# Placeholder products pinned behind the causal-mask products, and the first unit's maximum queued ahead of the second's

## Chip, cores and metric

The kernel runs on one core of a Trainium2 chip. The metric is device microseconds of one execution, from launch to end; three executions of the kernel before took 603.52, 604.0 and 604.48 us (median 604.0). Everything else comes from one profiled execution, in which the hardware recorded each instruction of each engine.

## What is computed

Causal attention, then two feed-forward stages, all in float32 precision:

```python
scores = scale * q @ k.T                       # 2 batches, 12 heads, 448 rows, head size 64
scores = where(upper triangle, -1e9, scores)   # causal mask
attn = exp(scores - rowmax) / (rowsum + 1e-9)
x = (attn @ v), heads side by side             # 896 x 768
h = x @ w_in; g = piecewise-quadratic(h); y = g @ w_out        # inner width 2048
out = (silu(y @ w_gate) * (y @ w_val)) @ w_out2                # inner width 1536
```

## The kernel before

The program is written in the order of a software pipeline, and a planner (the framework's scheduler) turns it into one instruction queue for each engine. An engine takes its queue strictly in order. The planner moves an instruction ahead of earlier written ones when, by its own estimate of time, the engine would stand idle otherwise. Two things limit it: an instruction that reads or overwrites data of an earlier one stays behind that one, and `tc.keep_in_program_order(op)` keeps `op` behind whatever was written last for the same engine. The helper `follow` (line 78) issues a product that way, at raised priority, unless its second argument (`first`) is true.

Attention is cut into units of two heads. For the first 12 steps (`j == 0`) a step is one unit's first 224 query rows; later steps (`j == 2`, `3`) take the rest, two steps a unit. The loop at line 505 runs over `k`, and each pass issues pieces of four neighbouring steps in the order of the table `ORDER` (line 54). In the first 12 passes the list is: `scores(k+1)`, `greatest(k+1)` (the word `max`), the filler, `values(k-2)`, `normalize(k)`, `turn(k-1)`, `exps(k+1)`; the copy `turned(k-2)` stands at the head.

- `scores` (line 338), on TensorE: four float32 products of queries and keys (each is two records of the profile), then four bf16 products of the mask with an identity (lines 353 to 359), which add the mask to the diagonal blocks. They read `mask_b`, made by GpSimd at line 481, and `ident_b`, made by VectorE at line 485. The result lies in one of two PSUM tiles `s`, so that `scores(k+2)` has to wait until `exps(k)` has read `scores(k)`.
- `greatest` (line 362), on VectorE: two row maxima and one multiplication by -1/8.
- `exps` (line 374), on ScalarE: four exponentials, each followed by a read of its row sums.
- `normalize` (line 388), on VectorE; `turn` (line 410), six transposes on TensorE; `turned` (line 420), a copy on ScalarE; `values` (line 429), the products with v on TensorE; `x_hi` and `x_lo`, the split of their result.

TensorE has nothing useful as filler in the first passes. `zeros(n)` (line 471) then issues `n` products of a zero tile into a PSUM bank that nobody reads (line 473): `zeros(WARM)` gives eight ahead of everything else, and passes k = 0 to 13 give 12, 6, 4 and then 2 each (`HOLD`, line 31), 44 in all. They are written without a pin. From pass 14 on the filler is a quarter of a real product of the first feed-forward stage. Weights arrive as two int32 halves of a float64 and are narrowed by three VectorE instructions (lines 99 to 105) before they are split in two (lines 195 and 196); the first two tiles' first instruction is pinned.

A step's scores products are called S0, S1, ... in this text, its mask products M0, M1, ..., its transposes T0, ..., its products with v V0, ...

Of the kernel before, what the change touches and what calls it, by code (L numbers as in the profile page):

```python
# [13 lines left out]
ALU = mybir.AluOpType  # L14
AX = mybir.AxisListType
# [6 lines left out]
C = 112  # L22
# [5 lines left out]
HALF = DM // 2  # L28
WB = 768
WARM = 8  # L30
HOLD = (12, 6, 4, 2)
AHEAD = 3
LASTB = 2
WBUFS = 4
# [29 lines left out]
def fused_kernel(ctx: ExitStack, tc: tile.TileContext, qk, v, w_in, w_out, w_gv, w_o2, out):  # L64
    nc = tc.nc
# [12 lines left out]
    def follow(product, first, *args, **kw):  # L78

        if first:  # L80
            return product(*args, **kw)  # L81
        with tc.high_priority():
            return tc.keep_in_program_order(product(*args, **kw))  # L83
# [178 lines left out]
    def bank():  # L262
        pool = banks.pop(0)
        banks.append(pool)
        return pool.tile([128, 512], F32, tag="mm", name="mm")
# [46 lines left out]
    with ExitStack() as ph:  # L312
# [25 lines left out]
        def scores(k):  # L338

            u, j = steps[k]  # L340
            qk_t, _ = ld[u]
            s = ps_s.tile([128, 2, 512], F32, tag="s", name="s")
            k0 = GT if j == 0 else 0

            for i, (off, w, q0) in enumerate(reversed(SEGS[j])):
                for h in range(2):
                    hd = slice(h * D, (h + 1) * D)
                    follow(
                        nc.tensor.matmul, i == h == 0,
                        out=s[:C, h, off:off + w], lhsT=qk_t[hd, q0:q0 + C], rhs=qk_t[hd, k0:k0 + w],  # L350
                        start=(i == 0), stop=False, skip_group_check=True,
                    )
            for off, w, _ in SEGS[j]:
                for h in range(2):
                    follow(
                        nc.tensor.matmul, False,
                        out=s[:C, h, off + w - C:off + w], lhsT=ident_b[:C, :], rhs=mask_b[:C, :],
                        start=False, stop=True, skip_group_check=True,
                    )
            st[k] = {"s": s}  # L360

        def greatest(k):

            _, j = steps[k]
            s, segs = st[k]["s"], SEGS[j]
            mx = s[:C, 0, 504:508].rearrange("p (i h) -> p i h", h=2)
            for i, (off, w, _) in enumerate(segs):
                nc.vector.tensor_reduce(out=mx[:, i], in_=s[:C, :, off:off + w], axis=AX.X, op=ALU.max)  # L368
            m = pp.tile([C, 2, 2], F32, tag="mx", name="mx")
            nc.vector.tensor_scalar(  # L370
                out=m[:, :len(segs)], in0=mx[:, :len(segs)], scalar1=-0.125, scalar2=None, op0=ALU.mult)
            st[k]["mx"] = m

        def exps(k):

            _, j = steps[k]
            s, mx = st[k]["s"], st[k]["mx"]
            sm = pp.tile([C, 2, 2], F32, tag="sm", name="sm")
            p = pp.tile([C, 2, S], F32, tag="p", name="p")
            for i, (off, w, _) in enumerate(SEGS[j]):  # L380
                for h in range(2):
                    nc.scalar.activation(  # L382
                        out=p[:, h, off:off + w], in_=s[:C, h, off:off + w], func=AF.Exp,
                        bias=mx[:, i, h:h + 1], scale=0.125, accum_out=sm[:, i, h:h + 1],
                    )
            st[k].update(p=p, sm=sm)

        def normalize(k):
            _, j = steps[k]
            p, segs = st[k]["p"], SEGS[j]  # L390
            sm = st[k].pop("sm")
            m = sm[:, :len(segs)]
            nc.vector.tensor_scalar(out=m, in0=m, scalar1=1e-9, scalar2=None, op0=ALU.add)
            nc.vector.reciprocal(out=m, in_=m)
            for i, (off, w, _) in enumerate(segs):
                if j == 0 and NORM_P:
                    nc.gpsimd.tensor_tensor(
                        out=p[:, :, off:off + w], in0=p[:, :, off:off + w],
                        in1=sm[:, i].unsqueeze(2).to_broadcast([C, 2, w]), op=ALU.mult,
                    )  # L400
                else:
                    norms = NORM0 if j == 0 else NORM1
                    for h in range(2):
                        ph, r = p[:, h, off:off + w], sm[:, i, h:h + 1]
                        if norms[(2 * k + h) % len(norms)] == "V":
                            nc.vector.tensor_scalar(out=ph, in0=ph, scalar1=r, scalar2=None, op0=ALU.mult)  # L406
                        else:
                            nc.scalar.mul(out=ph, in_=ph, mul=r)

        def turn(k):  # L410
            u, j = steps[k]
            p = st[k]["p"]
            t = ps_t.tile([128, 2, 512], F32, tag="t", name="t")
            for h in range(2):
                for i in range(NK[j]):
                    sl = slice(i * C, (i + 1) * C)
                    follow(nc.tensor.transpose, i == 0, t[:C, h, sl], p[:, h, sl], ident[:C, :C])
            st[k]["t"] = t

        def turned(k):  # L420
            u, j = steps[k]
            if j != 3:
                pts[u] = pp.tile([C, 2, 784], F32, tag="pt", name="pt", bufs=2)
            off, w = (336 if j == 3 else 0), NK[j] * C
            turns = TURN0 if j == 0 else TURN1
            (nc.vector.tensor_copy if turns[k % len(turns)] == "V" else nc.scalar.copy)(
                out=pts[u][:, :, off:off + w], in_=st[k].pop("t")[:C, :, :w])
# [30 lines left out]
        def x_hi(o, xh, xl):  # L458
            nc.scalar.copy(out=xh, in_=o)
            return o, xh, xl  # L460
# [6 lines left out]
        idle = lp.tile([128, 512], BF16, name="idle", bufs=1)  # L467
        nc.vector.memset(idle, 0.0)
        warm = bank()

        def zeros(n):
            for _ in range(n):
                nc.tensor.matmul(out=warm, lhsT=idle[:, :128], rhs=idle, start=True, stop=True)  # L473

        zeros(WARM)
        make_identity(nc, ident)
        nc.vector.memset(mask_b, 0.0)
# [4 lines left out]
            out=mask_b[:C, :], in_=mask_b[:C, :], compare_op=ALU.is_ge, fill=MASK,  # L482
# [22 lines left out]
        for k in range(-1, last + 2):  # L505
            lead, lag = k + 1 < last, k - 2 >= 0
            pv = lag and steps[k - 2][1] != 2
            kind = 0 if k < first1 else 2 + (k - first1) % 2
            for op in ORDER[kind]:
                if op == "copy" and lag:  # L510
                    turned(k - 2)
                elif op == "scores" and lead:
                    scores(k + 1)
                elif op == "max" and lead:
                    greatest(k + 1)
                elif op == "exp" and lead:
                    exps(k + 1)
                elif op == "norm" and 0 <= k < last:
                    normalize(k)
                elif op == "turn" and 0 <= k - 1 < last:  # L520
                    assert "t" not in st.get(k - 2, ())
                    turn(k - 1)
                elif op == "values" and pv:
                    assert not fresh_o and not half_o and "t" not in st[k - 2]
                    fresh_o.append(values(k - 2))
                elif op == "x_hi" and fresh_o:
                    half_o.append(x_hi(*fresh_o.pop()))
                elif op == "x_lo" and half_o:
                    x_lo(*half_o.pop())
                elif op == "fill" and k >= 0:  # L530
                    if k >= first1 + 2:
                        filler()
                    else:
                        zeros(HOLD[min(k, len(HOLD) - 1)])
                elif op == "relu" and fresh:
                    half.append(h_relu(*fresh.pop()))
                elif op == "square" and half:
                    whole.append(h_max(*half.pop()))
                elif op == "g_hi" and whole:
                    split_h.append(g_hi(*whole.pop()))  # L540
                elif op == "g_lo" and split_h:
                    g_lo(*split_h.pop())
                elif op == "weights" and k >= 2:
                    W.tick((TICKS if k < first1 else LATER)[k % 3])
            if lead and steps[k + 1][1] != 3:
                load(steps[k + 1][0] + AHEAD)
            if k == 0:
                W.load(2)
# [191 lines left out]
    for hf in range(2):  # L740
# [14 lines left out]
        for i in range(last):  # L755
            w = W.get(I_O2 + hf * NB + i)
# [58 lines left out]
```

## Time and profile before

| | |
|---|---|
| median of three executions | 604.0 us (603.52 to 604.48) |
| profiled execution, its own time | 603.42 us |
| its span, first to last instruction | 601.6 us |
| TensorE (PE) busy | 593.4 us, 99% |
| TensorE weight load (PEld) busy | 521.3 us, 87% |
| VectorE (DVE) busy | 441.5 us, 73% |
| ScalarE (ACT) busy | 232.4 us, 39% |
| attention passes | about 4.7 to 140 us of the span |

Times in the rows below are in us from the start of the span, durations in us unless ns is written. A timeline row gives the start, the duration, the engine, the line, the operation, output and inputs by name, shapes, and how many instructions were merged into it. Matmuls overlap in the pipeline, so a record's duration is longer than the distance to the next one's start; the pace is read from the starts. Products issued through `follow` carry line 81 or 83 (the helper), the zero products line 473.

### The profile page before, as it was taken

Reading aid. Unit: us, or ns where it says so; the run is one execution under the profiler, and the core shown is the slowest. Engines: PE = TensorE matmul, PEld = TensorE weight load, DVE = VectorE, ACT = ScalarE, POOL = GpSimd, SP = SyncE. Lnnn points to the kernel's source line nnn. Section 1 sums busy time; section 2 is a strip of 40 time slices with the busy share of each in tenths; the row PEclk is TensorE's granted clock in tenths of the full one; section 3 lists DMA queues with packets and bytes.
Section 4 is the critical chain, followed back from the end, with each engine's and each line's share of the span. In section 5 each row is a group of like instructions: output and inputs, shape, how many; then the busy total and the mean of one; then the engine's idle time right before and its main releaser. Section 6 shows DMA issues by size and latency. Waiting matters only on the chain.

```text
span 601.6 us, 8762 instructions
## 1 busy us (share of the span) xinstructions
PE 593.4 (99%) x3334; PEld 521.3 (87%) x3334; DVE 441.5 (73%) x811; ACT 232.4 (39%) x499; POOL 117.1 (19%) x68
## 2 busy tenths in 40 slices
PE   9999999999999999999999999999999999999997
PEld 5766667668999999999999999999999999999997
DVE  3999999872886777666874699489787899863401
ACT  3987777653344433111121454224224342512100
POOL 0000000000311221323133212124122233632300
PEclk9999999999999999999999999999999999999999
DMA  8575554300151234567644303133333333544002
GB/s 260 175 212 171 172 176 151 106 1 1 53 158 33 84 93 150 182 210 245 194 133 146 106 1 105 53 105 106 103 111 103 105 106 115 200 157 145 1 1 92
DMA packets 23417, 72.52 MB, mean 121 GB/s; under 512 B 2640, under 2 KB 9616, under 8 KB 23376
## 3 DMA queue, kind: packets, MB, share of 16 engines
q1 hardware_dynamic: 20784, 69.61, 36.7%
q10 hardware_dynamic: 2592, 2.36, 1.1%
q8 instruction: 26, 0.43, 0.3%
q14 instruction: 15, 0.12, 0.1%
HBM read 66.85 MB, written 5.11 MB: 120 GB/s over the span
## 4 chain that ended last, share of the span: by engine, by line
PE 84%; DVE 13%; ACT 1%; DMA 1%; issue 0%; ACTq 0%
PE mm L81 34%; PE mm L660 27%; PE mm L749 5%; PE mm L751 5%; PE mm L750 5%; DVE s L368 3%; DVE p L406 2%; PE mm L83 2%; PE s L81 1%; DVE wt L105 1%; DVE wt L102 1%; PE mm L473 1%; ACT p L382 1%; DVE wl L196 1%; DMA wraw<-w_in 1%; PE t L83 1%
## 5 line engine op out<-in xcount | busy, mean ns | idle before, releaser
L196 POOL TENSOR_TENSOR wl<-wt,wh 128x768 fp32r<-128x768 f32 (+1 forms) x52 | 102.5, 1976 | 428.3 <-ACT wh L195 428.3
L195 ACT CAST wh<-wt 128x768 fp32r<-128x768 f32 (+1 forms) x61 | 49.7, 816 | 152.0 <-DVE wt L105 40.7
L99 DVE TENSOR_SCALAR wt<-wraw 128x768 int32<-128x768 int32 (+1 forms) x64 | 44.9, 701 | 41.8 <-POOL wl L196 36.7
L102 DVE SCALAR_TENSOR_TENSOR wt<-wraw,wt 128x768 int32<-128x768 int32 (+1 forms) x64 | 72.5, 1132 | 0.8
L81 PE MATMUL mm<-gh,wh 128*128 128x448 f32 x192 | 70.1, 365 | 0.0
L81 PE MATMUL mm<-gh,wl 128*128 128x448 f32 x192 | 70.1, 365 | 0.0
L81 PE MATMUL mm<-gl,wh 128*128 128x448 f32 x192 | 70.1, 365 | 0.0
L660 PE MATMUL mm<-yl,wh 128*128 128x448 f32 x180 | 65.7, 365 | 0.0
L660 PE MATMUL mm<-yh,wl 128*128 128x448 f32 x180 | 65.7, 365 | 0.0
L660 PE MATMUL mm<-yh,wh 128*128 128x448 f32 x180 | 65.7, 365 | 0.0
L105 DVE SCALAR_TENSOR_TENSOR wt<-wraw,wt 128x768 int32<-128x768 int32 (+1 forms) x64 | 64.4, 1007 | 0.7
L81 PE MATMUL mm<-xh,wh 128*128 128x448 f32 x165 | 62.6, 379 | 2.4 <-DVE q L288 2.4
L749 PE MATMUL mm<-wh,uh 128*128 128x384 f32 x168 | 56.1, 334 | 0.0
L750 PE MATMUL mm<-wl,uh 128*128 128x384 f32 x168 | 56.1, 334 | 0.0
L751 PE MATMUL mm<-wh,ul 128*128 128x384 f32 x168 | 56.1, 334 | 0.0
L382 ACT ACTIVATE p<-s,mx 112x112 f32<-112x112 f32 (+3 forms) x96 | 46.4, 497 | 20.0 <-DVE mx L370 14.4
L81 PE MATMUL mm<-xl,wh 128*128 128x448 f32 x138 | 50.4, 365 | 0.0
L81 PE MATMUL mm<-xh,wl 128*128 128x448 f32 x138 | 50.2, 365 | 0.0
L368 DVE TENSOR_REDUCE s<-s 112x2 f32<-112x224 f32 (+3 forms) x48 | 35.4, 743 | 6.9 <-PE s L83 6.7
L81 PEld LDWEIGHTS mm<-gl,wh 128*128 128x128 f32 x192 | 36.1, 188 | 2.9
L81 PEld LDWEIGHTS mm<-gh,wl 128*128 128x128 f32 x192 | 36.1, 188 | 2.9
L81 PEld LDWEIGHTS mm<-gh,wh 128*128 128x128 f32 x192 | 36.1, 188 | 2.8
(132 smaller groups left out, 1216.8 us busy)
## 6 DMA issues: line engine op xcount, KB each, us to landing
wraw<-w_gv SPq DMA_DIRECT2D x18, 768.0 KB, 4.3
wraw<-w_in SPq DMA_DIRECT2D x16, 768.0 KB, 4.7
wraw<-w_out SPq DMA_DIRECT2D x12, 768.0 KB, 4.6
wraw<-w_o SPq DMA_DIRECT2D x12, 768.0 KB, 4.2
araw<-w_gv SPq DMA_DIRECT2D x18, 256.0 KB, 4.8
qk_t<-qk SPq DMA_DIRECT2D x12, 336.0 KB, 3.2
wraw<-w_out SPq DMA_DIRECT2D x6, 512.0 KB, 3.8
qk_t<-qk SPq DMA_DIRECT2D x12, 224.0 KB, 3.9
```

The costliest lines, as they stand in the source:

```text
L81: return product(*args, **kw)
L99: yield nc.vector.tensor_scalar(out=t, in0=w[:, :, 1], scalar1=3, scalar2=0x3FFFFFF8, op0=ALU.logical_shift_left, op1=ALU.bitwise_and,)
L102: yield nc.vector.scalar_tensor_tensor(out=t, in0=w[:, :, 1], scalar=-0x40000000, in1=t, op0=ALU.bitwise_and, op1=ALU.bitwise_or,)
L105: yield nc.vector.scalar_tensor_tensor(out=t, in0=w[:, :, 0], scalar=29, in1=t, op0=ALU.logical_shift_right, op1=ALU.bitwise_or,)
L195: nc.scalar.copy(out=wh[:, :n], in_=t)
L196: (nc.vector if i < LOW_V else nc.gpsimd).tensor_tensor(out=wl[:, :n], in0=t, in1=wh[:, :n].bitcast(F32), op=ALU.subtract,)
L368: nc.vector.tensor_reduce(out=mx[:, i], in_=s[:C, :, off:off + w], axis=AX.X, op=ALU.max)
L382: nc.scalar.activation(out=p[:, h, off:off + w], in_=s[:C, h, off:off + w], func=AF.Exp, bias=mx[:, i, h:h + 1], scale=0.125, accum_out=sm ...
L660: nc.tensor.matmul(out=ps[:, :N], lhsT=w[a][:, sl], rhs=rows[c][b], start=(first and c == i == 0), stop=(last and c == i == 2), skip_group ...
L749: nc.tensor.matmul(out=ps, lhsT=c, rhs=a, start=(f == 0), stop=False)
L750: nc.tensor.matmul(out=ps, lhsT=c, rhs=b, start=False, stop=False)
L751: nc.tensor.matmul(out=ps, lhsT=d, rhs=a, start=False, stop=(f == FC2 - 1))
```

## The change

`HOLD` gives 9 instead of 12 zero products in pass 0. The zero products of passes 0, 1 and 2 are pinned in program order: nine behind M1, six behind M2, four behind M3. The first product of S1 is pinned too, so that all of S1 lies behind M0. The maxima and the negation of steps 0 and 1 are pinned on VectorE, in the order written.

```diff
-HOLD = (12, 6, 4, 2)
+HOLD = (9, 6, 4, 2)
...
                     follow(
-                        nc.tensor.matmul, i == h == 0,
+                        nc.tensor.matmul, i == h == 0 and k != 1,
                         out=s[:C, h, off:off + w], lhsT=qk_t[hd, q0:q0 + C], rhs=qk_t[hd, k0:k0 + w],
...
             for i, (off, w, _) in enumerate(segs):
-                nc.vector.tensor_reduce(out=mx[:, i], in_=s[:C, :, off:off + w], axis=AX.X, op=ALU.max)
+                largest = nc.vector.tensor_reduce(out=mx[:, i], in_=s[:C, :, off:off + w], axis=AX.X, op=ALU.max)
+                if k < 2:
+                    tc.keep_in_program_order(largest)
             m = pp.tile([C, 2, 2], F32, tag="mx", name="mx")
-            nc.vector.tensor_scalar(
+            negate = nc.vector.tensor_scalar(
                 out=m[:, :len(segs)], in0=mx[:, :len(segs)], scalar1=-0.125, scalar2=None, op0=ALU.mult)
+            if k < 2:
+                tc.keep_in_program_order(negate)
...
-        def zeros(n):
+        def zeros(n, pin=False):
             for _ in range(n):
-                nc.tensor.matmul(out=warm, lhsT=idle[:, :128], rhs=idle, start=True, stop=True)
+                op = nc.tensor.matmul(out=warm, lhsT=idle[:, :128], rhs=idle, start=True, stop=True)
+                if pin:
+                    tc.keep_in_program_order(op)
...
-                        zeros(HOLD[min(k, len(HOLD) - 1)])
+                        zeros(HOLD[min(k, len(HOLD) - 1)], k < len(HOLD) - 1)
```

## Rows read from the trace of the kernel before

**Rows 1.** View by windows: stretch, length, PE, PEld, DVE, ACT, POOL busy, clock, DMA, GB/s.

```profile
5.00:16.00 11.00, 11.00 (x90) 7.00 (x89) 5.74 (x23) 4.99 (x24) 0.00 (x0) 1.00 0.92 300
16.00:63.00 47.00, 46.72 (x394) 31.46 (x392) 46.67 (x151) 39.94 (x134) 0.00 (x0) 1.00 0.63 195
63.00:112.00 49.00, 47.60 (x328) 32.71 (x327) 48.57 (x120) 34.44 (x81) 0.00 (x0) 1.00 0.50 151
112.00:145.00 33.00, 31.16 (x212) 22.98 (x212) 19.88 (x51) 17.87 (x43) 0.00 (x0) 1.00 0.08 25
145.00:597.00 452.00, 452.00 (x2304) 424.96 (x2303) 319.43 (x464) 133.65 (x220) 116.14 (x61) 1.00 0.35 112
```

**Rows 2.** The same view for the zero products alone: PE, PEld, clock, DMA, GB/s.

```profile
0.00:5.00 5.00, 3.60 (x8) 1.04 (x8) 1.00 0.53 143
5.00:12.00 7.00, 5.47 (x24) 2.22 (x24) 1.00 1.01 337
12.00:20.00 8.00, 0.04 (x1) 0.00 (x0) 1.00 0.63 193
```

**Rows 3.** Timeline of TensorE, 4.7 to 12 us.

```profile
4.71 0.50 PE L81 MATMUL s<-qk_t 64*112 64x224 f32 x1
...
5.51 0.44 PE L81 MATMUL s<-qk_t 64*112 64x224 f32 x1
...
6.28 1.68 PE L473 MATMUL mm<-idle 128*128 128x512 bf16 x7
7.80 0.58 PE L83 MATMUL s<-mask_b,ident_b 112*112 112x112 bf16 x8
...
8.21 3.83 PE L473 MATMUL mm<-idle 128*128 128x512 bf16 x17
```

**Rows 4.** Timeline of VectorE and ScalarE in the same stretch; in brackets, what ended idle time.

```profile
8.36 1.76 DVE L368 TENSOR_REDUCE s<-s 112x2 f32<-112x224 f32 x4 [6.75 <-PE s L83]
10.03 0.29 DVE L370 TENSOR_SCALAR mx<-s 112x4 f32<-112x4 f32 x2
10.28 0.35 ACT L382 ACTIVATE p<-s,mx 112x112 f32<-112x112 f32 x1 [8.05 <-DVE mx L370]
...
11.95 0.17 DVE L393 TENSOR_SCALAR sm<-sm 112x4 f32<-112x4 f32 x1 [1.64 <-ACT p L382]
```

**Rows 5.** Timeline of GpSimd and VectorE: the last writers of the mask products' operands.

```profile
1.26 0.28 POOL L481 TENSOR_SCALAR_AFFINE_SELECT mask_b<-mask_b 112x112 bf16<-112x112 bf16 x1
1.34 0.28 DVE L485 CAST ident_b<-ident 128x112 bf16<-128x112 f32 x1
```

**Rows 6.** Timeline of TensorE, 11.9 to 20 us: first rows of S2, M2, T0, S3, S4, S5.

```profile
11.97 0.44 PE L81 MATMUL s<-qk_t 64*112 64x224 f32 x1
...
12.73 0.41 PE L83 MATMUL s<-mask_b,ident_b 112*112 112x112 bf16 x4
12.98 0.27 PE L81 MATMUL t<-ident,p 112*112 112x112 f32 x1
...
13.76 0.44 PE L81 MATMUL s<-qk_t 64*112 64x224 f32 x1
...
16.59 0.44 PE L81 MATMUL s<-qk_t 64*112 64x224 f32 x1 [0.23 <-ACT p L382]
...
19.18 0.44 PE L81 MATMUL s<-qk_t 64*112 64x224 f32 x1
```

**Rows 7.** Timeline of ScalarE and VectorE: copy of T0, exponentials of step 2, weight narrowing.

```profile
13.86 0.72 ACT L426 COPY pt<-t 112x672 f32<-112x672 f32 x1 [0.41 <-PE t L83]
...
14.90 0.35 ACT L382 ACTIVATE p<-s,mx 112x112 f32<-112x112 f32 x1 [0.32 <-DVE mx L370]
...
16.72 0.55 DVE L99 TENSOR_SCALAR wt<-wraw 128x768 int32<-128x768 int32 x1
...
18.72 0.95 DVE L102 SCALAR_TENSOR_TENSOR wt<-wraw,wt 128x768 int32<-128x768 int32 x1
```

**Rows 8.** DMA issues from 0 to 6.2 us: KB, median us to landing.

```profile
wraw<-w_in SPq DMA_DIRECT2D x1, 768.0 KB, 6.7
```

## The prediction, made before the changed kernel was run

> **What bounds the kernel now.** The view by windows comes first, with one question: where does TensorE stand idle at all? From 145 to 597 us it is busy for 452.00 of 452.00 us, so whatever the attention passes gain or lose by 145 us reaches the end undiminished [rows 1]. Before that its idle time is small: nothing from 5 to 16 us, 0.28 us from 16 to 63, 1.40 from 63 to 112, 1.84 from 112 to 145 [rows 1]. That is 3.52 us between 5 us and the end of the dense part. VectorE is nearly as full from 16 us on (46.67 of 47.00 us to 63, [rows 1]), so the two pace each other, but an instruction added to TensorE's queue has almost no gap to fall into. I therefore keep an account: the time is TensorE's work plus TensorE's waits.
>
> Some of that work is not real. Of the 44 zero products behind the first eight, 24 run from 5 to 12 us, none starts from 12 to 20 us, and the last 20 come after that [rows 2]. The timeline of the start shows what the 24 lie beside [rows 3, 4]: S0 and S1 start at 4.71 and 5.51, seven zeros at 6.28, the eight mask products of both steps only at 7.80, then seventeen zeros from 8.21 until S2 at 11.97 [rows 6]. Meanwhile VectorE waits for the mask until 8.36, does all four maxima, and ScalarE's first exponential starts at 10.28 [rows 4]. So the seven zeros delay the start chain, and the seventeen fill the wait that the chain causes.
>
> **The change part by part.** *Seven zeros leave the place ahead of the masks, and M0 goes ahead of S1.* The operands of the mask products are written by 1.54 and 1.62 us [rows 5], so M0 should be able to start where S0 ends, at 5.51. Four mask products occupy 0.25 us ahead of transposes (12.73 to 12.98, [rows 6]); I allow 0.29. S1 then runs from 5.80 for 0.77 us (5.51 to 6.28, [rows 3]), M1 until 6.86.
>
> *The maximum of step 0 goes first.* The maxima began 0.15 us after the mask products' slot ended (8.21 to 8.36, [rows 3, 4]), so at 5.95 now. Four maxima took 1.67 us to the first negation at 10.03, two take 0.84; the exponentials began 0.25 after that negation [rows 4]: 5.95 + 0.84 + 0.25 = 7.04. S2 followed the first exponential by 1.69 us (10.28 to 11.97, [rows 4, 6]), so its PSUM tile is free at 8.73. The second pair of maxima and its negation (about 1 us) now lies beside those exponentials, and costs nothing there.
>
> *Nine zeros between M1 and S2.* Seventeen took 8.21 to 11.97, 0.221 us each [rows 3, 6]; nine take 1.99: 6.86 to 8.85. They cover the wait for the exponentials and end 0.12 us behind it. **S2 starts at 8.85 instead of 11.97, 3.12 us earlier.**
>
> *Ten zeros enter a stretch that had none.* Six are pinned behind M2 and four behind M3, where the queue before went M2, T0, S3, M3, V0 and TensorE had no idle time [rows 1, 6]. TensorE's order is fixed, so T0 and V0 must wait for them although their inputs may be ready. The two zeros of pass 3, unpinned, were among the 24 as well; they write the same bank as the pinned ones and cannot run before them, so they come at their written place, behind S4. That is 12 more by S5, 12 x 0.221 = 2.65 us. The walk: S2 8.85, M2 9.61, six zeros from 9.9, T0 11.2, S3 at 12.0 (0.78 us behind T0's start, as 12.98 to 13.76), M3 12.8, four zeros, V0 at 14.0, T1, S4 at about 15.4 (2.60 us of work lay between S3 and S4 before, 2.83 less the wait of 0.23), two zeros, S5 at about 18.5. Before, S3, S4 and S5 were at 13.76, 16.59 and 19.18 [rows 6].
>
> *Who waits behind the pinned zeros?* ScalarE: its copy of T0 came 0.10 us behind T0's end and took 0.72 us (13.86, [rows 7]). It moves to about 12.1 and is done before V0's turn. Should the exponentials of step 2 (1.67 us, if as those of step 0 from 10.28 to 11.95, [rows 4]) stand behind this copy in ScalarE's queue, they end by about 14.6, still ahead of S4 at 15.4. Thus the 0.23 us that TensorE waited for them before S4 [rows 6] goes too. VectorE waits idle for M3 and M4; it starts normalizing at about 8.7 instead of 11.95 [rows 4], so it has some 2 us to spare.
>
> *The queue of SyncE.* Loads of q and k wait for the step that frees their tile; S1 ends 0.3 us later than before, S2 three earlier, and none of the loads is needed within that. The first weight tile, issued at 6.03, landed 6.7 us later, at about 12.7 [rows 8]; its narrowing stood at 16.72 [rows 7] and is kept behind the negation of step 3, now at about 14.2. So it has 1.5 us to spare.
>
> *The sum.* By the walk: 3.12 - 2.65 + 0.23 = 0.70 us. By the account: three zeros fewer (0.66) and the wait of 0.23, 0.89 us; the difference is four mask products more in the place of a single block of eight. I take **0.8 us**. The profiled execution would go from 603.42 to 602.6; the median of 604.0 lies 0.6 above that execution, so the forecast for it is **603.2 us**. What comes earlier by 3.1 us is mostly given back because twelve zeros that ran for free now run where TensorE has no free time.
>
> **A rule weighed against this.** TensorE's busy rows read full in all these stretches, and the four products of a step take the same time whether others wait for them or not: 0.80 us in S0, 0.77 in S1, 0.76 in S2 [rows 3, 6]. The Trainium skill, on the page Perfetto Trace Analysis, section Identifying the Most-Contended Engine, holds that matmul busy time is a poor measure for TensorE and that the busy share of weight loads is a better one. By that measure it has room here: 31.46 of 47.00 us from 16 to 63, against 424.96 of 452.00 later [rows 1]. If that room is slack, the sum would be 3.1 us instead of 0.8.
>
> **The rivals.**
>
> *VectorE gets ahead.* With 2.4 us more head start than TensorE (3.2 against 0.8) VectorE could do weight narrowing early, two instructions of 0.95 us a tile [rows 7], if the planner moves them there. Then TensorE's waits from 63 to 112 us (1.40 us, [rows 1]) shrink: 0.8 + up to 1.4, **601.8 to 602.7**. For it: VectorE is full from 16 to 112 us. Against: it can't go ahead of scores that TensorE has not made.
>
> *Hidden zeros.* If TensorE's full rows hold slack and VectorE alone sets the pace to 112 us, its earlier start of 3.1 us stays: **601.0**. Against: equal distances between products in steps with and without waiting partners, as above.
>
> *The waits come back.* The planner orders all that is not pinned by its own estimate, and that estimate changes. If TensorE's waits from 63 to 145 us grow by 0.8 to 1.6 us, which is up to half as much again, nothing or a little less than nothing is left: **604.0 to 604.8**. This is also the case in which the change doesn't do what it says.
>
> *M0 doesn't start early (slower).* The trace never shows a mask product ready before 7.80. Were something else than the zeros holding it there, S1, now pinned behind M0, and all zeros would stand behind it: M0 7.80, S1 8.1, M1 8.9, nine zeros until 11.2, S2 at 11.2, only 0.8 us earlier, against 2.65 us of zeros and 0.23 regained: 1.6 us lost, **605.6**. It decides from an M0 start of about 6.2 on. Against: the operands' writers are done six us earlier [rows 5].
>
> *The clock falls (slower).* The first eight zeros took 0.45 us each, the next ones 0.22, though the granted clock reads 1.00, its upper level of 2.4 GHz, in every stretch [rows 2, 3]. If the matmuls from S2 to S3 ran at the slow pace again, 3.1 us would double: **606.3**. Against: from 12 to 20 us no zero ran, only scores, transposes and values, at 1.00 [rows 1, 2]; the new queue spreads zeros over just that stretch. The Trainium skill, page TensorE: Matmul & The Clock Gate, section Part 4: PE-mode transpose, says that transposes don't count as activity for the clock; the rows, where the transposes take 0.78 us of a step of 2.59 (T0; S4 to S5), show no fall.
>
> **How the numbers follow.** Forecast (602.9 to 603.5) 0.47; VectorE ahead 0.24; hidden zeros 0.10; waits come back 0.09; M0 late 0.06; clock 0.04. A measurement of this kernel can tell about 0.2%, 1.2 us, from no change: faster means below 602.8, slower above 605.2. Faster is 0.24 + 0.10 = 0.34, the same 0.47 + 0.09 = 0.56, slower 0.06 + 0.04 = 0.10. The range runs from 601.3, which leaves out hidden zeros, to 604.8, which leaves out both slower cases: 0.2 outside. The likeliest case's own range is 602.9 to 603.5.
>
> **What would show it.** In the profile after: M0 at about 5.5, first exponential at about 7.0, S2 at 8.7 to 8.9 with no idle time of TensorE before it; six and four zeros behind M2 and M3; S5 at about 18.5; TensorE busy about 0.7 us less in all. A TensorE gap before S2, or T0 starting before the six zeros, would break the walk; S5 as early as 16.1 would speak for hidden zeros; equal S5 but less idle time from 63 to 145 us for VectorE ahead.

## Result and the profile after

The changed kernel takes 611.43 us (median of 22 executions, 603.89 to 611.97), the kernel before, run beside it, 603.63 us (22 executions, 603.25 to 610.94). The ratio after to before is 1.0099, with a 95% interval from 1.0076 to 1.0122. The change makes the kernel about 1% slower.

The executions do not spread evenly. Of the 22 of the changed kernel, 19 lie between 610.7 and 612.0 us and three between 603.8 and 605.0; of the kernel before, 20 lie between 603.2 and 606.1 and two at 610.3 and 610.9. The profiled execution of the changed kernel belongs to its large group: 611.42 us, span 609.6 us, against 603.42 and 601.6 before. So 8.00 us are to be found, and then it is to be explained why three executions do not have them.

**Where TensorE stands idle.** The view by windows of the kernel after; the columns are those of [rows 1].

```profile
5.00:16.00 11.00, 10.43 (x86) 6.69 (x85) 7.51 (x29) 5.80 (x27) 0.00 (x0) 1.00 0.94 310
16.00:63.00 47.00, 45.98 (x378) 31.05 (x377) 46.59 (x147) 38.68 (x129) 0.00 (x0) 1.00 0.62 192
63.00:112.00 49.00, 47.56 (x330) 32.16 (x329) 48.93 (x116) 33.32 (x80) 0.00 (x0) 1.00 0.50 167
112.00:145.00 33.00, 31.11 (x223) 23.22 (x223) 19.60 (x54) 18.35 (x43) 0.00 (x0) 1.00 0.01 1
155.00:597.00 442.00, 442.00 (x2214) 408.60 (x2213) 309.65 (x457) 129.59 (x213) 112.69 (x61) 1.00 0.35 113
```

Idle time of TensorE from 5 to 145 us is 0.57 + 1.02 + 1.44 + 1.89 = 4.92 us, against 3.52 before. The granted clock reads 1.00 in every stretch, its upper level of 2.4 GHz. From 155 to 597 us TensorE is busy all the time, as before [rows 1]. By these rows alone the change would cost about a microsecond, and eight are to be explained.

**Where the eight microseconds are.** The chain of work that ended last shows it. The columns are the start, the length, engine, tile, line and how many instructions; first the last pieces of the kernel before, then of the kernel after.

```profile
145.81 200.79 PE mm L81 x990
346.60 164.16 PE mm L660 x810
```

```profile
146.68 204.69 PE mm L81 x990
351.38 167.40 PE mm L666 x810
```

The dense part starts 0.87 us later (146.68 against 145.81). Then the same 990 products take 3.90 us longer and the same 810 another 3.24 us (line 660 has become line 666, with the lines that the change adds). That is 0.87 + 3.90 + 3.24 = 8.01 us, the whole difference. Each product got slower by about the same amount: 3.90/990 is 3.9 ns, 3.24/810 is 4.0 ns. TensorE is busy without a gap there in both kernels; it simply starts fewer products in the same time. The view by windows for TensorE alone (busy time, instructions, clock, share and rate of the DMAs), one stretch of 25 us in the middle, before and after:

```profile
300.00:325.00 25.00, 25.00 (x125) 1.00 0.48 149
```

```profile
300.00:325.00 25.00, 25.00 (x123) 1.00 0.43 136
```

Both are full, both at clock 1.00, and one holds two products less. A busy share cannot show this; a count of instructions can. Taken from the starts in the trace, the mean distance between the products 128x448 is 202.67 ns before and 206.67 ns after, and each holds from about 149 us to the end of that row (at 511 us before, 519 after), over 1788 products: 1788 x 4.0 ns = 7.15 us.

**Where the pace begins.** The timeline of TensorE around the last irregular place ahead of that stretch, the kernel before and the kernel after:

```profile
147.47 0.37 PE L81 MATMUL mm<-xh,wh 128*128 128x448 f32 x1
147.68 0.36 PE L81 MATMUL mm<-xl,wh 128*128 128x448 f32 x1
147.92 0.47 PE L81 MATMUL mm<-xh,wh 128*128 128x448 f32 x1
148.23 0.37 PE L81 MATMUL mm<-xl,wh 128*128 128x448 f32 x1
148.43 0.36 PE L81 MATMUL mm<-xh,wl 128*128 128x448 f32 x1
148.63 0.37 PE L81 MATMUL mm<-xh,wh 128*128 128x448 f32 x1
```

```profile
148.34 0.37 PE L81 MATMUL mm<-xh,wh 128*128 128x448 f32 x1
148.55 0.36 PE L81 MATMUL mm<-xl,wh 128*128 128x448 f32 x1
148.79 0.47 PE L81 MATMUL mm<-xh,wh 128*128 128x448 f32 x1
149.10 0.36 PE L81 MATMUL mm<-xl,wh 128*128 128x448 f32 x1
149.30 0.37 PE L81 MATMUL mm<-xh,wl 128*128 128x448 f32 x1
149.51 0.37 PE L81 MATMUL mm<-xh,wh 128*128 128x448 f32 x1
```

Up to 148.55 us the kernel after keeps the same distances as the other (0.20). At 148.79 (147.92 in the kernel before) both have a small stumble, 0.24 and then 0.31 us, and behind it the paces part. The weight load of that product shows why there is one; PEld, before and after:

```profile
147.92 0.19 PEld L81 LDWEIGHTS mm<-xh,wh 128*128 128x128 f32 x1 [0.26 <-DVE q L288]
```

```profile
148.79 0.19 PEld L81 LDWEIGHTS mm<-xh,wh 128*128 128x128 f32 x1 [0.25 <-DVE q L288]
```

The load that elsewhere runs one product ahead waited 0.25 us for VectorE, which was emptying a PSUM bank. It is the last wait for another engine, of TensorE or of its loads, before that row ends. From then on TensorE waits for nobody, and the pace stays.

**The attention passes of the kernel after.** The timeline of TensorE at the start; line 477 holds the zeros.

```profile
4.71 0.71 PE L81 MATMUL s<-qk_t 64*112 64x224 f32 x1
...
5.73 0.41 PE L83 MATMUL s<-mask_b,ident_b 112*112 112x112 bf16 x4
6.08 0.83 PE L83 MATMUL s<-qk_t 64*112 64x224 f32 x8
6.83 0.41 PE L83 MATMUL s<-mask_b,ident_b 112*112 112x112 bf16 x4
7.08 2.11 PE L477 MATMUL mm<-idle 128*128 128x512 bf16 x9
9.23 0.44 PE L81 MATMUL s<-qk_t 64*112 64x224 f32 x1
...
10.24 1.46 PE L477 MATMUL mm<-idle 128*128 128x512 bf16 x6
11.54 0.26 PE L81 MATMUL t<-ident,p 112*112 112x112 f32 x1
...
12.21 0.44 PE L81 MATMUL s<-qk_t 64*112 64x224 f32 x1
...
13.22 1.03 PE L477 MATMUL mm<-idle 128*128 128x512 bf16 x4
14.77 0.40 PE L81 MATMUL o<-pt,v_t 112*64 112x224 f32 x1 [0.53 <-ACT pt L430]
...
17.22 0.60 PE L477 MATMUL mm<-idle 128*128 128x512 bf16 x2
17.75 0.44 PE L81 MATMUL s<-qk_t 64*112 64x224 f32 x1
```

VectorE and ScalarE in the same stretch (the first maxima and their negation, the first exponential, the first of step 2, the copy of T0):

```profile
6.18 1.06 DVE L368 TENSOR_REDUCE s<-s 112x2 f32<-112x224 f32 x2 [4.57 <-PE s L83]
7.28 0.16 DVE L372 TENSOR_SCALAR mx<-s 112x4 f32<-112x4 f32 x1
```

```profile
7.54 0.35 ACT L386 ACTIVATE p<-s,mx 112x112 f32<-112x112 f32 x1 [5.32 <-DVE mx L372]
...
12.47 0.35 ACT L386 ACTIVATE p<-s,mx 112x112 f32<-112x112 f32 x1 [1.76 <-DVE mx L372]
...
13.99 0.73 ACT L430 COPY pt<-t 112x672 f32<-112x672 f32 x1
```

The start does what it says: M0 at 5.73 instead of 7.80, S2 at 9.23 instead of 11.97 [rows 3, 6], 2.74 us earlier. Then V0 waits 0.53 us, because ScalarE takes the exponentials of step 2 (12.47 to 13.99) ahead of the copy of T0; in the kernel before the copy came first, at 13.86 [rows 7].

How long the gain lives is told by the starts of the scores of each step, counted from the same products in both traces (us; the third line is after less before):

```
step      S2     S5     S8     S11    S12    S14    S16    S19    S26    S35
before  11.97  19.18  28.81  37.09  40.28  46.09  51.42  64.81  92.35 128.36
after    9.23  17.75  27.44  35.93  40.20  49.19  54.33  65.54  93.30 129.22
        -2.74  -1.43  -1.37  -1.16  -0.08  +3.10  +2.91  +0.73  +0.95  +0.86
```

At S11 1.16 us are left. Two rows of TensorE's timeline name what takes them away:

```profile
38.38 1.89 PE L477 MATMUL mm<-idle 128*128 128x512 bf16 x8
...
54.33 0.53 PE L81 MATMUL s<-qk_t 64*112 64x336 f32 x1 [0.79 <-ACT p L386]
```

Eight zeros stand in one place ahead of S12, and S16 waits 0.79 us for exponentials. None of this is written in the change: those zeros and steps are not pinned, and the planner ordered them anew. What is left at the end is +0.87 us. The account comes near it: 1.40 us more waits, less three zeros (0.66), are 0.74; the rest is small and was not separated (the mask products stand in two blocks instead of one, and S0 ran slower in this trace).

### The profile page after: what moved, and what is told of

The parts are those of the page before. It is cut to its first block, busy times and chain, and to the rows that moved or that the text cites. A ratio compares the mean times of both kernels' runs of the same rounds, so it can differ in the third digit from the quotient of the medians.

```text
span 609.6 us, 8756 instructions
## 1 busy us (share of the span) xinstructions
PE 600.0 (98%) x3331; PEld 520.8 (85%) x3331; DVE 437.9 (72%) x811; ACT 231.7 (38%) x499; POOL 115.1 (19%) x68
## 4 chain that ended last, share of the span: by engine, by line
PE 85%; DVE 12%; ACT 3%; issue 0%; ACTq 0%; DVEq 0%
PE mm L81 34%; PE mm L666 27%; PE mm L756 5%; PE mm L757 5%; PE mm L755 5%; DVE s L368 3%; DVE p L410 2%; ACT p L386 2%; PE mm L83 2%; PE s L81 2%; DVE wt L105 1%; DVE wt L102 1%; PE o L81 1%; PE mm L477 1%; PE t L83 1%; PE s L83 1%
## 5 line engine op out<-in xcount | busy, mean ns | idle before, releaser
L196 POOL TENSOR_TENSOR wl<-wt,wh 128x768 fp32r<-128x768 f32 (+1 forms) x52 | 100.8, 1941 | 436.9 <-ACT wh L195 433.6
L99 DVE TENSOR_SCALAR wt<-wraw 128x768 int32<-128x768 int32 (+1 forms) x64 | 41.8, 654 | 46.9 <-POOL wl L196 45.6
L102 DVE SCALAR_TENSOR_TENSOR wt<-wraw,wt 128x768 int32<-128x768 int32 (+1 forms) x64 | 70.8, 1107 | 0.8
L105 DVE SCALAR_TENSOR_TENSOR wt<-wraw,wt 128x768 int32<-128x768 int32 (+1 forms) x64 | 62.9, 982 | 0.7
```

Of the source, the lines that this page charges most:

```text
L99: yield nc.vector.tensor_scalar(out=t, in0=w[:, :, 1], scalar1=3, scalar2=0x3FFFFFF8, op0=ALU.logical_shift_left, op1=ALU.bitwise_and,)
L102: yield nc.vector.scalar_tensor_tensor(out=t, in0=w[:, :, 1], scalar=-0x40000000, in1=t, op0=ALU.bitwise_and, op1=ALU.bitwise_or,)
L105: yield nc.vector.scalar_tensor_tensor(out=t, in0=w[:, :, 0], scalar=29, in1=t, op0=ALU.logical_shift_right, op1=ALU.bitwise_or,)
L196: (nc.vector if i < LOW_V else nc.gpsimd).tensor_tensor(out=wl[:, :n], in0=t, in1=wh[:, :n].bitcast(F32), op=ALU.subtract,)
```

## Experiments

Two questions were tested. First the dense part. *The first theory* says that a long unbroken row of 128x448 products holds one of two paces, that it takes one at its last interruption and keeps it, and that the change only moved that interruption. Its rivals say that the slow pace belongs to the changed kernel itself (where its tiles lie, what its queues hold), or to the chip's condition in that execution. Second the attention passes: what took the 2.74 us.

For the first question the kernels get an extra product, narrower than 448 columns, ahead of chosen chunks of the first feed-forward stage. It writes the chunk's own PSUM bank, which the next product starts afresh, so the result is the same; it only breaks the row.

```diff
         ps = bank()
+        w = NUDGES.get((g, f), 0)
+        if w:
+            follow(nc.tensor.matmul, True, out=ps[:, :w], lhsT=wh[:, :128], rhs=xh[:, 0, :w], start=True, stop=True)
```

**A ladder of interruptions in the kernel after.** Twenty such products, 32 to 448 columns wide, one each ahead of twenty of the 23 last chunks of that stage; nineteen of them lie behind the last wait.

> The changed kernel with a short extra product (32 to 448 columns, its result overwritten at once) ahead of 19 of the 23 chunks of 18 products that open the long TensorE stretch. Theory 1, two paces: the 128x448 products hold one of two paces, 202.7 or 206.7 ns, taken at the last interruption; then segments between the extra products show either pace, several of each, and only a product ahead of a chunk changes it. Theory 2, the changed kernel's tiles or queues make its products slow: every segment stays at 206.7 ns. Theory 3, the clock: the pace falls at one time and stays, whatever the chunk. Cost of the extra products themselves: 19 times 0.1 to 0.3 us, 2 to 6 us; total 604.5 + 4 plus up to 7.2 us by the last pace.

It took 612.45 us. The mean distances, worked out from the starts in the trace, by segment (start in us, products, width of the product ahead of it, mean distance in ns, the first two distances left out because they still show the interruption):

```
153.63  18  128  202.67        191.39  18  288  206.20
157.42  18  192  202.67        195.26  18  352  206.67
161.19  18  256  202.73        199.16  18  416  202.67
164.99  18  320  202.67        202.83  55   64  202.67   (holds the 448-wide one)
168.82  36  384  202.64        214.12  18  128  202.67
176.14  18   32  202.67        217.90  18  192  206.67
179.90  18   96  206.67        221.76  18  256  206.67
183.76  18  160  206.67        225.50  18   48  202.67
187.61  18  224  202.67        229.26 1404  80  206.66
```

There is nothing between the two values (at 191.39 us the first distances are 203, 205, 205 and 202 ns, then the upper value holds), and a segment keeps what it starts with, be it 18 products or 1404. Both paces stand in one execution of one kernel, a few us apart, so neither the chip's condition nor the kernel as a whole can be the cause. The width does not decide it by itself: 192 and 256 columns were followed once by the lower and once by the upper distance. The clock reads 1.00 there too.

**The same ladder in the kernel before.**

> The same extra products in the kernel before, which ran its long stretch at 202.7 ns. Theory 1: here too some segments take 206.7 ns, and the same widths tend to give the same pace as in the changed kernel. Theory 2: all segments stay at 202.7 ns.

It took 612.5 us, and the eighteen segments have the same distances in the same order: 206.67 at 180.12, 183.97, 195.48, 218.12, 221.98 and for the last 1404 products, 206.27 at 191.60, the lower value elsewhere. With the same interruptions both kernels run at the same pace. That a pace is taken at an interruption and kept held; that the slow pace needs the changed kernel's tiles or queues fell. That the change did no more than move an interruption is not shown by this.

**One interruption, meant to make the kernel after quick** (64 columns ahead of one chunk at the end of attention):

```diff
+NUDGES = {(1, 1): 64}
```

> The changed kernel with one extra product of 64 columns ahead of the second chunk of the long stretch. In the ladders a 64 or 32 column product was followed by 202.7 ns each time. Theory 1 (the pace is taken at the last interruption): all executions lie at 604.2 to 605.2 us, the changed kernel's 611.4 is gone, since 1766 products at 4.0 ns less are 7.1 us. Theory 2 (the kernel's tiles or queues make its products slow): still 611 to 612.

Ten executions: nine between 604.0 and 605.1 us, one at 611.36; median 604.83, ratio to the kernel before 1.0012 (0.9977 to 1.0047). The expectation, all of them quick, was missed by that one. It is the profiled one, and its long row shows 206.67 ns from 148.53 us. The trace also shows that the extra product lay at about 146.3 us, ahead of the last wait and not behind it. So it did not itself set the pace; it altered the interruption behind it, where the weight load now waits 0.35 us instead of 0.25. By their times, 1 of 10 executions is slow with it, where the kernel after has 19 of 22.

**The same product in the kernel before.**

> The kernel before with the same extra product. Theory 1: 603.4 to 604.0 us in every execution, without the rare ones near 610; it costs 0.2 us itself. fast_after minus fast_before is then what the change does to attention alone: 0.9 us slower by the starts of the long stretch (148.79 and 147.92).

604.26 us (603.34 to 605.55, ten executions), ratio 1.0007 (0.9996 to 1.0018). The product itself costs nothing that can be measured. None of the ten was near 610, but six lie above the 604.0 that was expected as the upper end, and the medians of the two kernels with this product differ by 0.57 us, where 0.9 was expected.

**Meant to make the kernel before slow** (the ladder's last two products alone):

```diff
+NUDGES = {(0, 15): 48, (1, 15): 80}
```

> The kernel before with two extra products, 48 and 80 columns, ahead of the last two chunks of the first feed-forward stage. In the ladders 80 columns behind 48 gave 206.7 ns for all 1403 products that followed. Theory 1: 603.5 + 0.3 + 1403 x 4.0 ns = 609.4 us, the kernel before made slow without any part of the change. Theory 2: 603.8.

The expectation was missed: 604.14 us (603.35 to 605.36, ten executions). In its trace the distances are 202.67 ns up to the 48 columns, 206.67 for one chunk behind them and 202.66 for the 1404 products behind the 80 columns. In the ladder the same two products had given the two paces the other way round. So the same width does not always give the same pace, and the two products flipped it twice. That suggested to leave out the second.

**One product of 48 columns in the kernel before.**

```diff
+NUDGES = {(0, 15): 48}
```

> The kernel before with one extra product of 48 columns ahead of chunk 15 (first half) of the first feed-forward stage, at about 223 us. With 80 columns behind it this one was followed by 18 products at 206.7 ns. Theory 1 (two paces, held from interruption to interruption): all 1421 products behind it stay at 206.7 ns, 603.5 + 0.1 + 1421 x 4.0 ns = 609.3 us, in most executions, with no part of the change in it. Theory 2 (placement): 603.6 us. Theory 3, the pace drifts back by itself: something between.

609.85 us, ratio 1.0099 (1.0082 to 1.0116): four of five executions between 609.4 and 610.1, one at 604.38. This is the kernel before with its attention untouched, and one extra product of 48 columns makes it slower by as much as the change did. The profiled execution was the one at 604.38. Its timeline shows how small the interruption is: the two products at 223.27 us take the place of one, and the next distance is 0.20 again.

```profile
223.06 0.37 PE L82 MATMUL mm<-xh,wl 128*128 128x448 f32 x1
223.27 0.47 PE L82 MATMUL mm<-xh,wh 128*128 128x48 f32 x2
223.58 0.36 PE L82 MATMUL mm<-xl,wh 128*128 128x448 f32 x1
223.77 0.36 PE L82 MATMUL mm<-xh,wl 128*128 128x448 f32 x1
```

In that execution 202.67 ns held ahead of it and behind it. A slow execution of this kernel was not profiled; by the first theory the 1421 products behind the 48 columns at 4.0 ns more would cost 5.7 us, and the four executions lie 5.1 to 5.7 above the one; a row slow from 149 us on would have cost 7.2. That these four were slow behind the 48 columns is thus concluded from their times.

**Attention: the copy of T0 ahead of the exponentials of step 2.** The rest as in the kernel after.

```diff
                 if op == "copy" and lag:
                     turned(k - 2)
+                    if k == 2:
+                        exps(2, True)        # each exponential pinned
...
-                elif op == "exp" and lead:
+                elif op == "exp" and lead and k != 1:
```

> The changed kernel with ScalarE's copy of T0 kept ahead of the exponentials of step 2. If the order of these two cost the wait ahead of V0, TensorE's 0.53 us there vanishes, V0 starts at 14.0 to 14.2 instead of 14.77, and the long stretch begins 0.3 to 0.6 us earlier than 148.79 us. Rival: the wait moves to S4 or S5 behind the later exponentials, and the stretch begins within 0.2 us of 148.79. The total says nothing by itself, since it holds either pace.

604.32 us, long row at 202.67 ns. The copy moved to 12.58 us and the exponentials behind it, and V0 starts at 14.44 without a wait (14.0 to 14.2 was expected). But the last interruption comes at 148.83 us, as late as in the kernel after (148.79); the expected gain of 0.3 to 0.6 us did not show. S5 is at 19.35 instead of 17.75, while S19 is at 62.16 instead of 65.54 and S21 again 0.19 later. The wait before V0 is not what lost the 2.74 us, since a gain or loss of two or three us comes and goes between S5 and S21.

**Attention: no zeros behind the first nine.**

```diff
-HOLD = (9, 6, 4, 2)
+HOLD = (9, 0, 0, 0)
```

> The changed kernel with HOLD (9, 0, 0, 0): the nine zero products stay, the other 32 are left out. By the account of TensorE's work each costs 0.22 us, so the long stretch would begin up to 7 us earlier than 148.79 us, less what VectorE (46.6 of 47 us busy from 16 to 63 us) takes back; estimate 2 us earlier. If zeros are hidden behind VectorE: within 0.5 us of 148.79. If the zeros hold the clock up: the granted clock reads below 1.00 from 10 to 45 us and the stretch begins later.

601.91 us. Thirty-two zeros are gone, 7.0 us of TensorE's work, and the last interruption moves from 148.79 to 146.42 us, 2.37 earlier. So two thirds of the zeros lay in time that TensorE would have waited anyway. S4 is 2.47 us ahead of the kernel before and S7 still 2.48; then S8 is 1.04 ahead and S12 0.57, though TensorE has no idle time from 23 to 28 us: other work now stands ahead of S8 in its queue. No zero starts after 9.2 us, and the clock stays at its upper level; the view by windows, TensorE alone:

```profile
16.00:63.00 47.00, 43.62 (x356) 1.00 0.61 190
63.00:112.00 49.00, 48.15 (x336) 1.00 0.48 151
```

TensorE's idle time from 16 to 63 us grows to 3.38 us, from 1.02 in the kernel after, and the whole is still quicker.

**Attention: only the zeros without a pin left out, and only the pinned ones of passes 1 and 2.**

```diff
-HOLD = (9, 6, 4, 2)
+HOLD = (9, 6, 4, 0)
```

> The changed kernel without the 22 unpinned zero products of passes 3 to 13; the ten pinned ones stay. If the unpinned ones, eight of which stand in one place ahead of S12, cost what the change lost between S11 and S19, the long stretch begins 1 to 2 us earlier than 148.79 us, about as in the run without all late zeros (146.42). If VectorE sets the pace there, within 0.5 us of 148.79.

603.64 us; the last interruption at 148.15, 0.64 us ahead of the kernel after. It lies between what was expected of the two cases (1 to 2 us, or within 0.5) and decides nothing.

```diff
-HOLD = (9, 6, 4, 2)
+HOLD = (9, 0, 0, 2)
```

> The changed kernel without the ten pinned zeros behind M2 and M3; the 22 unpinned ones stay. By the account the ten cost 2.2 us: S5 at 15.5 to 16.0 instead of 17.75 us, and the long stretch 2.2 us earlier, 146.6. If later waits take it back, S5 early but the long stretch within 0.5 us of 148.79.

602.58 us; the last interruption at 147.09, 1.70 us ahead of the kernel after and 0.83 ahead of the kernel before. S5 starts at 16.92 (15.5 to 16.0 was expected) and S12 at 37.42, 2.86 us ahead of the kernel before. Here the early start does live through the twelve short passes. The ten pinned zeros are 2.2 us of work, and leaving them out gives 1.7 us. From 2.74 us ahead at S2 to 0.87 behind at the end, attention lost 3.6 us; the ten are about half of that.

**Attention: the other pins without those of the zeros.**

```diff
-HOLD = (9, 6, 4, 2)
+HOLD = (12, 6, 4, 2)
...
-                        zeros(HOLD[min(k, len(HOLD) - 1)], k < len(HOLD) - 1)
+                        zeros(HOLD[min(k, len(HOLD) - 1)])
```

> The changed kernel with the zero products unpinned and 12 in pass 0, as before: M0 ahead of S1 and the first maximum ahead of the second are left. The planner now puts eleven zeros ahead of M0. M0 at about 8.2 us, first exponential about 9.6 instead of 7.54 (before 10.28), S2 at about 11.3. If the pins of the zeros carried the earlier start, the gain of 2.74 us at S2 falls to about 0.7.

605.71 us, the last interruption at 150.19. TensorE's timeline at the start:

```profile
4.71 0.71 PE L81 MATMUL s<-qk_t 64*112 64x224 f32 x1
...
6.11 3.01 PE L477 MATMUL mm<-idle 128*128 128x512 bf16 x12
8.96 0.37 PE L83 MATMUL s<-mask_b,ident_b 112*112 112x112 bf16 x4
9.26 0.83 PE L83 MATMUL s<-qk_t 64*112 64x224 f32 x8
10.02 0.41 PE L83 MATMUL s<-mask_b,ident_b 112*112 112x112 bf16 x4
10.27 1.89 PE L477 MATMUL mm<-idle 128*128 128x512 bf16 x8
12.42 0.44 PE L81 MATMUL s<-qk_t 64*112 64x224 f32 x1 [0.26 <-ACT p L386]
```

The planner puts twelve zeros ahead of M0, and S2 comes at 12.42, later than before the change (11.97, [rows 6]), where 11.3 was expected. Part of this is not the edit. In this execution S0 and the first two zeros still ran slow: 1.40 us from S0 to the first zero, where S1 to the zeros took 0.77 before [rows 3], and 0.40 and 0.29 us for two zeros instead of 0.22 each. That is 0.9 us; without it S2 would come at about 11.5 by estimate, 0.4 ahead of the kernel before. So the pins of the zeros carry most of the early start. That the other pins alone make it worse is not shown.

**A version that is quicker than both:** nine pinned zeros, none later, and the 64-column product.

```diff
-HOLD = (9, 6, 4, 2)
+HOLD = (9, 0, 0, 0)
+NUDGES = {(1, 1): 64}
```

> The changed kernel without its 32 late zero products and with the 64 column product. The long stretch began 2.4 us earlier than in the changed kernel and 1.5 earlier than before: 601.9 + 0.2, 601.8 to 602.3 us in every execution, faster than both kernels by the removal of zeros and the held pace.

602.43 us (601.52 to 602.69, seven executions), ratio to the kernel before 0.9973 (0.9962 to 0.9984). None was slow. Seven executions do not show that none ever will be, and what the product adds is not shown either: without it the kernel took 601.91 us in its one execution. Five of the seven lie outside the expected 601.8 to 602.3.

One caution on all attention figures. TensorE's first products run at half the pace (zeros 0.43 us apart instead of 0.22), as at the lower of its clock's two levels, 1.2 GHz, and the moment at which this ends differs between executions. The trace's record of the granted clock begins at that moment, with 1.00: at 4.86 us in the kernel before, at 5.28 in the kernel after, from 3.93 to 6.92 in all the traces. The views read 1.00 ahead of it too, where there is no record. In the trace of the kernel before with 48 and 80 columns, the latest, S1 was still slow; before, its first row was 0.44 us long [rows 3].

```profile
5.96 0.58 PE L82 MATMUL s<-qk_t 64*112 64x224 f32 x1
```

S2 is 0.84 us later there than in the kernel before (12.81), and so is the last wait (148.76 against 147.92), with the same attention. It is better, then, to count from the start of M0. To the last wait it is 143.05, 143.06 and 143.08 us in the three traces with the attention of the kernel after (after, one interruption, ladder), and 140.05 to 140.57 in the five with that of the kernel before. By this count the copy ahead of the exponentials gains 0.22 us, leaving out the unpinned zeros 0.40, the ten pinned ones 1.53, all late zeros 2.40. The last two are clear of the scatter, the first two are not. Of the +0.87 of the change, 0.2 us is the later clock (from S0 to M0 1.02 us, from S0 to S1 0.80 before); the other 0.65 is little more than the 0.52 us between the five traces.

## Why the prediction was wrong, and where it was right

**The step that failed** stands in the first paragraph of the prediction: since TensorE is busy for 452.00 of 452.00 us, "whatever the attention passes gain or lose by 145 us reaches the end undiminished". It treats the length of the dense part as a constant. It is not: TensorE is busy for all of it in both kernels, and 1788 products take 7.15 us longer in one. The clock rival came nearest, a slower TensorE at 606.3, but at another place and by another way: the granted clock reads 1.00 in all the rows of after. The zeros of 0.45 us on which it rested are no second pace at clock 1.00 either: the clock record of that trace begins only behind them. No rival had the dense part in it, and the range ended at 604.8.

Could the trace of before have shown it? The long row has one pace throughout, 202.67 ns. But the fillers of the attention passes are groups of six products of the same shape, and in the trace of before 4 of 24 such groups settle at 206.67 ns, starting at 76.71, 101.04, 124.76 and 132.92 us (7 of 23 in the kernel after). The second pace was there to see for anyone who compared distances within one shape. What the change would make of it was not there to see.

**The early start was right.** M0 does start without its zeros, at 5.73 us. S0 to M0 took 1.02 us instead of the 0.80 that S0 to S1 had taken: its first records at 4.71 are 0.71 us long, where those of S0 before were 0.50 [rows 3], since the clock rose 0.42 us later in this execution. Two maxima took 1.10 us to the negation (6.18 to 7.28), not half of 1.67. Together with the maxima's start, 6.18 instead of 5.95, the first exponential came at 7.54 instead of 7.04. From there the step held to the digit: S2 1.69 us behind it, at 9.23 (forecast 8.85).

**The walk to S5 was right in size and wrong in its order.** Six zeros took 1.30 us (10.24 to 11.54; 1.33 reckoned), T0 came at 11.54 (11.2), S3 at 12.21 (12.0). V0 came at 14.77 instead of 14.0, since the exponentials of step 2 stood ahead of the copy in ScalarE's queue, the opposite of the order that the prediction considered. S5 came at 17.75 instead of 18.5, because the planner put it ahead of V1. S8 and S11, 1.37 and 1.16 us ahead, are better than the 0.8 of the sum.

**The waits came back.** This rival (604.0 to 604.8) had 0.09, and by its size it is what attention did: TensorE's idle time grew by 1.40 us, and the last interruption comes 0.87 us later. The place was another: the rival had the waits grow from 63 to 145 us, where they grew by 0.09 us (3.24 to 3.33); the other 1.31 came from 5 to 63 us, where the walk had counted on regaining 0.23. The wait of 0.53 before V0 and that of 0.79 at S16 are the larger ones. The executions of the kernel after at the quick pace, 603.89, 604.71 and 604.92 us, lie in or next to its range. So without the second pace the change would have been no gain either, where 0.8 us was forecast. The price of the ten pinned zeros was right in kind (1.5 to 1.7 us measured by leaving them out, 2.2 reckoned). What was missing is that the planner reorders everything that has no pin as soon as the times ahead of it move: eight zeros ahead of S12 and S14 to S16 three us late, far from any line of the diff.

**Hidden zeros** (601.0, chance 0.10) is half true. Leaving out 7.0 us of zeros gave 2.4 us, so most of them lay beside waits for VectorE and ScalarE; the rows of TensorE's idle time can't tell that, since a zero fills the very gap that it would have shown. The Trainium skill's page Perfetto Trace Analysis, section Identifying the Most-Contended Engine, which distrusts the busy share of matmuls and looks at that of weight loads, pointed the right way here: 31.46 of 47.00 us had said that there was room [rows 1].

**What stays open.** That the pace is taken at an interruption and kept is shown. What in the last nanoseconds decides between the two is not: the first distances behind it are 310, 203 and 199 ns in the profile of before, 313, 201 and 207 in that of after. Nor is it shown why, by their times, the kernel before meets the quick pace in 55 of the 58 executions measured beside these experiments and the kernel after in 3 of 22. The moment of the last wait alone does not decide: in the kernel before with narrow products at 223 us it came at 148.76 and 148.78 us and the quick pace followed, in the kernel after at 148.79 and the slow one did. Shown is only that these odds answer to the change and to one narrow product alike, so that the 7.15 us are not the price of the edit's own lines.

## What to carry to other kernels

Where an engine is busy without a gap, count its instructions in equal stretches and compare the starts of equal instructions: a full row says nothing of the pace. Before a loss is put down to what an edit did, look whether the times of the executions fall into groups, and let a harmless edit elsewhere (here one narrow product) show whether the time answers to that edit or merely to being disturbed. Before traces are compared, look where each comes up to speed; here that moved all that follows by up to 0.8 us. And with a planner, an edit's price near its own lines is only half of it: pins hold what they name, and everything behind them may be ordered anew.

## What the runs showed of the hardware

A long row of products 128x448 with a new 128x128 weight tile each runs at 202.67 or at 206.67 ns a product, 2% apart, at granted clock 1.00 in both cases. It keeps its pace over up to 1788 products, until something interrupts it; a weight load that waited 0.25 us, or one product of 48 columns, is enough to change it, and does not always. The Trainium skill, page TensorE: Matmul & The Clock Gate, section Back-to-back issue gap, gives an isolated product a 2.4th of a nanosecond for each column and 2.5 ns more, which would be 189 ns for 448 columns by estimate, and says that in a row of loads and products both set the distance. Neither value here is 189. The weight loads have the same length in both kernels (188 ns in the profile's pages), and the products 128x384 of the last stage keep one distance (173.4 ns before, 173.3 after).

TensorE's granted clock read 1.00 from 16 to 112 us also in the kernel without any zeros behind the first nine, although TensorE stood idle for 3.38 of the 47 us to 63. At the start it rose between 3.93 and 6.92 us in the fourteen traces: in the earliest behind six zeros and a part of the seventh, in the latest behind eight zeros and nearly all the scores of S0 and S1. What sets the moment is open here.
